# Two products of the single-layer steps without an array position, and another order of the weight loads, in an interleaved two-layer transformer kernel

## The chip, the cores and the metric

The kernel runs on one core of one Trainium2 chip. The metric is the device time of one execution in microseconds (us). A core has a matrix engine (TensorE, PE in the profile; its weight loads are shown apart, as PEld), a vector engine (VectorE, DVE), an activation engine (ScalarE, ACT), a general engine (GpSimd, POOL) and a queue engine (SyncE, SP) that here issues most of the transfers.

## What is computed

Two layers, each an attention block with a recurrent memory and a gated FFN, run over 2048 rows of 576 numbers, with the same weights in both layers. The attention goes through 64 segments of 32 rows in sequence: eight memory rows are put in front of a segment, and the first eight rows of its output are the memory of the next.

```python
def _A_ref(x, mem0, Wq, Wk, Wv, Wo, seg_len):      # H = 32 heads of 128, M = 8
    mem = mem0
    for s in range(n_seg):                          # 64 segments of 32 rows
        h = concat([mem, x[s]])                     # 40 x 576
        q, k, v = h @ Wq, h @ Wk, h @ Wv            # per head, 40 x 128
        p = softmax(where(mask, q @ k.T * scale, -1e9))
        o = (p @ v) @ Wo                            # 40 x 576
        mem = o[:M]
        outs.append(o[M:])

x = x + _A_ref(_layernorm(x), ...)                  # layer 0
x = x + (silu(ln(x) @ w1) * (ln(x) @ w3)) @ w2      # 576 -> 4608 -> 576
x = x + _A_ref(_layernorm(x), ...)                  # layer 1
x = x + (silu(ln(x) @ w1) * (ln(x) @ w3)) @ w2
```

## The kernel before

**Steps.** The recurrence makes the segments of a layer sequential. So the kernel runs the two layers side by side, layer 1 eight segments behind (`LAG = 8`): step t holds segment t of layer 0 and segment t - 8 of layer 1. There are 72 steps, 0 to 71. In steps 8 to 63 there are two layers, and the moving operand of most products is 80 columns wide (2 x 40). In steps 0 to 7 and 64 to 71 there is one, and it is 40 columns wide: these sixteen are the single-layer steps. `both(t)` tells them apart.

**A step on TensorE.** The code gives each block of products a letter. Q and q are the query and key products of one of eight units of four heads, from the 512 first rows of the model dimension and from its last 64 (four blocks of 128 rows, and a rest of 64 rows, which the kernel calls the tail). V, v, X, x, G, g are the value products. S are the scores of one of four groups of eight heads, T the transposes of the probabilities, P the product with V, O and o the product with Wo: O its first 512 output columns (32 products of 128x128), o its last 64 (8 products with 128x64 weights). F, f, W, w belong to the FFN, whose work for a group of 128 rows of each layer is spread over the next four steps; a, b, p, n are transposes.

**Order.** Nothing is scheduled on the chip. `plan` (line 76) walks a list of nodes with estimated durations and fixes the order of each engine's instructions, which engine evicts a PSUM bank, and which bank or buffer each node gets. TensorE's order is not chosen there: three strings of letters, `FIRST` (steps 0 to 15), `FOUR` (four steps, used eleven times) and `LAST` (steps 60 to 71), give it. `plan` adds `SWITCH` = 0.098 to a TensorE node whose `mode` differs from that of the node before: `full` for products on the whole 128x128 array, `col` for those placed on halves of 64 columns, `row` for halves of 64 rows, and others.

**Scores and Wo's tail.** In a two-layer step, the scores of the two layers stand on the two column halves of the array (positions (0, 0) and (0, 64)). In a single-layer step there is one layer, and its scores, with weights of 40 columns, are at (0, 0). Wo's tail has 64 output columns; `wo_tail` (line 1033) puts the heads of a group by turns on the two column halves, so that each half sums four of the eight heads:

```python
r = R64 * (hl % 2)
self.mm(yT[r:r + R64, 4, :], self.T.WO[:, self.head(g, hl), 4 * P:D], OT[:, hl, :], False, ...,
        tile_position=(0, r))
```

The two sums are added later: ScalarE copies the odd half to `YO` (`y_odd`, line 1044, node `Yodd`), and VectorE adds it to the even half when it writes the memory's last 64 rows for the next step (`y_mem`, second part) and the segment's output (`yts`, second part). The first Q of the next step waits for the first part of `y_mem` alone; the first q also for the second part.

**Transfers.** All weights of the attention stay in SBUF: Wq and Wk in `W`, loaded in two halves of 16 heads (`load_qk`), Wv in `WV`, Wo in `WO`, in four quarters of eight heads. They are issued as Wq/Wk half 0, half 1, Wv, Wo (`ld_h`, `ld_v`, `ld_o`, lines 251 to 253, where the lower number goes first). FFN weights stream through two buffers each (`W13`, `W2C`) for every four steps. After step 71 one FFN for one row group is left (18 pairs of 128 hidden columns). For two of its pairs the weights are kept from the FFN before; the other sixteen are loaded by `tail_load` (line 686) over Wq and Wk in `W` and over Wv in `WV`, in eight pieces of two pairs. A piece waits for the Q and q products of step 71 that read its part of `W`, its second part for the last value products; pieces 4 to 7 wait for the O blocks of step 71 as well (`late`, line 467). One queue (SP) issues these transfers in the order of the plan, so a transfer that waits for a buffer holds back those behind it.

`qk` (line 869) has a detail that matters at the start: in step 0, for units 0 and 4, twelve wide products with the identity run first, if the unit's main block comes before its tail block.

Of the kernel before, what the change touches and what calls it, by code (L numbers as in the profile page):

```python
# [10 lines left out]
ALU = mybir.AluOpType  # L11
# [173 lines left out]
def ewh(*ns):  # L185
# [5 lines left out]
    "maQqqqQQSQqqqQTQSqqQSQSXxvVPTPTOPOTOoooPOoQQQqqVSqqvQQqqSQQqqSQTXPSxTOPTPOTOPoooOoaQQqqqqQSvQVSqQQqTQSqqQSPTPOOT"  # L191
    "ooPTPOOooQQqqqvqSVQQQqSTQqqQPSqQOSoTXPTOPTOPxooOoQQpQqqqqQSVSnvqQFffqFQQTSqqPQOToSfFPWTOPfFTOPFOfoooWQQfqqqQSvVF"
    "qfQFQWSqqQFSfQTQPqqfFOTSoWPFTOPfxXTFPOOoooWQQqqfqQQSfqFSvVfqqQFQWSqTQQPFqffTOSoPWOTFPFTOPfaOoooWQFQqqfQSVvqqfFQQ"
    "SqWQQqqqQSTPSTbOPoXTOPTxxPOOoooXqqQpQQqqSVvnQFFSfqQqfqQQTSqfFPQTOPSofWTOPFOTFPWOoooFQqqffQQqSQQQqqgqGTSWPQQfqqFF"
    "fgSSTGGPFgfTOWPOfgGTOPFOooooWQQfqqqFQvSfqFQQfqSVTFQqfFQPSaTWQPfqqFOSoTWFOPffFTOPWOoooFQqqqfQQSWQqqQQSqqTbQSGgqgQ"
    "PGTGPSggOTGPOTOPoooOoQQppqqVqqvSQQnnQFSfqfqFTQQPFSqqfQTwOPWFSoffTOFPwTOPWOoooFQffqqFQwWSQQFfqqfFTGqqgSQPQFWTQSgf"
    "qqGQwPFTSfggOGGPOTwPOOooooWFfqqQQFQqfqvVSQQWFfqqSQwTFPaSqfqQTQwFWPSffTOPFOOTwPWOooooFqqfqQQWqSQQQSqqqQQbQSqggGTG"
    "PGTSggPGTOPOTwPOOoooo"
)
FOUR = (  # L200
    "QqQpQpQqqqvVSSnnQFffqqFQQTFSffqqQPFTWSPOwTFPOTOPwOooooWQQqqqfQSQQQqqqfFGgfSSTFPFQqfqgGQTWwPFTSfggGFPGOTOPOOooooW"
    "wQQqqqfQFQvfqfVSSwFQWQFqffqFWTQPwTFSffqqQOPWoSwTFPFOTOPwWOoooffFQqqQWQSqqqQaQSbQQTQqqqgGSSgPGTGPOTggGPOTwPOOoooo"
)
LAST = (
    "QQpqqqQpSqqQQnVqvSnQTQQPqqSFTSffOPFOTFPfwTOPFOooooWQQqfqqQFwWSfqfQQFGSgfqqQTFPGwSTWFqfgqQQPWTFSfgfgGFwGPOTOPOOoo"
    "oofFWQwQFqfqqQQWSfqVvSQFTFqqfQPQTwSqqfFOQPWwffSFTFPOOTFPWOoooowQQqqqfQQSvqqqVSQWTQQPqqQOTSSbPwvVoXTOPToxPOOooVpp"
    "qqvQQQqqSQQnnQqqfSFQTFPSfqqQTFfSPOOwTWPFfTOPFOoooowQWfqqQQQFvqqfVSSFQQfqqFTWQfqqSQPwTOPoSXfTFPOWOTxfPFOwoooFQQvq"
    "fqVSqqQQWwFTQqfqfSQQPFwFqfqSQTWOPSfFTFWPOTOPwOooooffQFqqQWQSqqqQwFvSfVQTQPWqqQSOQqwTSbPOTXoPToxPOOooQqqqqQpQQSVv"
    "QnqSQFqfqfFQTQqSPSwTOPFFTffoPOTOPwOoooFQqqfqQQqfvSVFQFQSqfqQTQQqfqSFPSXTwPOTFPOTxooPOOoowQQqqvfSVqqqQQQSqQQTSfFP"
    "FTfqqQOoSPwTfOFPFTOPfooOowQQqqqqQSQQSqfqFQVvSfFTwQQqfqPTSFPFTOPOTOPwOooooffpFnwFfffFFFwffFFwfffFFwFwfffFFFwfffFF"  # L210
    "wFwFffffFFww"
# [11 lines left out]
def make_nodes(em, nseg, pools, o=Opt, dma_bw=230e3, load_bw=400e3):  # L223
# [27 lines left out]
    ld_h = [load("ldqk", kb(512 + 2 * R64, 4096), half - 9.0, em.load_qk(half)) for half in (0, 1)]  # L251
    ld_v = [load("ldv", kb(512 + 2 * R64, 4096), -7.0, em.load_v())]
    ld_o = [load("ldo", kb(1024, 576), g - 6.0, em.load_o(g)) for g in range(NG)]
# [45 lines left out]
    def v_nodes(name, t, k, prio, tail_at, emit, strips, deps, tail_deps, free):  # L299
# [6 lines left out]
        for r in (0, 1):  # L306
            outs = em.v_parts(strips, r)
            b[r].users = len(outs)
            for p0, width, row, blk in outs:
                e = node("AD", ew(512), em.v_ev(b[r], p0, width, row, blk), deps=[m_, n] + free.get(blk // 2, []), prio=prio + 0.01 * (blk // 2),  # L310
                         rel=[b[r]], name=name + "e")
                vx_ev.setdefault((name, t, blk // 2), []).append(e)
# [17 lines left out]
    def vg_out(t, g, b, deps, row):  # L330

        return [node("AD", ew(512), em.v_ev(b[r], row, R64, row, 2 * g + r), deps=deps, prio=t + o.vm + 0.01 * g + (0.05 if row == 0 else 0.0), rel=[b[r]],
                     name="VGe") for r in (0, 1)]
# [10 lines left out]
    def step(t):  # L344
# [17 lines left out]
        for g in range(NG):  # L362
# [18 lines left out]
            sc = node("PE", 8 * 0.0165 * nl, em.scores(t, g, qs, s), deps=qe, prio=pf + o.sc, mode="col", acq=[s, sme], rel=qs, name="SC")  # L381
# [26 lines left out]
            wot = node("PE", 4 * mm80, em.wo_tail(t, g, ot), deps=[wo], prio=t + o.wo + o.wog * g, mode="col", rel=[ot], name="WOt")  # L408
# [7 lines left out]
        if t == nst - 1:  # L416
            last_reads[2].extend(wos)
# [3 lines left out]
        yo = node("ACT", actc(c80), em.y_odd(t), deps=wots[3:], prio=t - 0.008, name="Yodd")  # L421
        if nxt:
            m = 8 * len(nxt)
            ye.append(node("ACT", actc(4 * m), em.y_mem(t, nxt, 0), deps=wos[3:] + wots, prio=t - 0.01, name="Ymem"))
            ye.append(node("DVE", dve(m, m), em.y_mem(t, nxt, 1), deps=[yo] + ye, prio=t - 0.005, name="Ymem"))
        ht_mem[t + 1] += ye
        yts = [node("ACT", actc(*([128] * nl)), em.yts(t, ls, 0), deps=wos[3:] + wots + ye, prio=t + 0.01, rel=[y], name="YTS")]
        yts.append(node("DVE", dve(*([32] * nl)), em.yts(t, ls, 1), deps=[yo] + yts, prio=t + 0.01, rel=[y], name="YTSt"))
# [12 lines left out]
    last_reads = [], [], []  # L441
    kept = {}

    def job(j):
# [18 lines left out]
        if last:  # L463
            v_done, qk_done, wo_done = last_reads
            tail = []
            for i in range(8):
                late = wo_done[i - 4:i - 3] if i >= 4 else []
                parts = [(0, 9 * 512, qk_done[2 * i:2 * i + 2] + late), (1, 4 * 576, v_done + late)]
                tail.append([load("tail", kb(128, c), s0 + o.tail_at + 0.01 * i, em.tail_load(i, what), deps=dep) for what, c, dep in parts])
# [89 lines left out]
class Emitter:  # L559
# [126 lines left out]
    def tail_load(self, i, what):  # L686

        def f(n):
            T = self.T
            fa = i * 512  # L690
            t13, t2 = T.W[:, :, fa:fa + 512], T.WV[:, i * 4 * D:(i + 1) * 4 * D].rearrange("p (b d) -> p b d", b=4)
# [610 lines left out]
```

## Time and profile before

| | before |
|---|---|
| median of three runs | 2702.27 us (2697.04 to 2702.94) |
| span of the profiled run | 2703.5 us, mean granted TensorE clock 0.992 |
| TensorE busy | 2629.8 us, 97% of the span |
| VectorE, ScalarE, GpSimd busy | 2089.3, 1370.6, 333.5 us |
| transfers | 321.40 MB, mean 119 GB/s |

The page gives busy times, and a chain: the work that ended last, followed back step by step to what released it. A timeline line has start, length, engine, line, operation, written and read tiles, weight shape, the shape of the moving operand and the number of instructions merged in it; a matmul's length includes the time in which the next ones already run, so the distance between starts is the time it costs. All matmuls are recorded by one helper (line 578), so the tile names tell the groups apart: `bank<-QKT` are scores, `bank<-OT,WO` with weights of 128*64 is Wo's tail, `bank<-HT,W` Q and q, `bank<-WV,HT` values, `bank<-XTB,W` and `bank<-W2C,HTT` or `bank<-WV,HTT` the FFN.

### The profile page before, as it was taken

What the parts mean: (1) busy time and instruction counts of PE and PEld (TensorE: products, weight loads), DVE (VectorE), ACT (ScalarE), POOL (GpSimd) and SP (SyncE); (2) the same over time, 40 slices, a digit from 0 to 9 for tenths busy, and PEclk for the clock granted to TensorE, in tenths of its full rate; (3) what the DMA queues carried; (4) which work ended last, traced back from release to release, by engine and by line L of the source; (5) the groups of instructions that cost most, each with busy time, mean ns of one, the idle gap of its engine ahead of it and who ended that gap; (6) DMA issues with size and microseconds to landing.
All of it is one profiled execution on the core that took longest, in us unless ns stands there. A gap on an engine that the chain in (4) does not pass through costs nothing.

```text
span 2703.5 us, 126553 instructions
## 1 busy us (share of the span) xinstructions
PE 2629.8 (97%) x55714; PEld 2227.4 (82%) x55795; DVE 2089.3 (77%) x5376; ACT 1370.6 (51%) x4025; POOL 333.5 (12%) x400
## 2 busy tenths in 40 slices
PE   5999999999999999999999999999999999999998
PEld 3788888888888888888888888888888888888886
DVE  4778887887778778777877877787787777787876
ACT  2655554544546454454645445464544546454553
POOL 1111110110101011010101101010110101011110
PEclk7999999999999999999999999999999999999999
DMA  9064534334343333434333343433334342434358
GB/s 316 4 176 120 158 89 119 88 110 125 93 131 88 115 92 110 125 95 130 87 114 93 110 125 93 131 88 112 94 110 125 93 131 71 125 97 135 117 164 258
DMA packets 483224, 321.40 MB, mean 119 GB/s; under 512 B 26376, under 2 KB 477328, under 8 KB 482160
## 3 DMA queue, kind: packets, MB, share of 16 engines
q1 hardware_dynamic: 479488, 306.22, 38.7%
q8 instruction: 436, 7.14, 1.1%
q0 software_dynamic: 3024, 6.93, 0.9%
q14 instruction: 116, 0.95, 0.1%
q10 hardware_dynamic: 160, 0.16, 0.0%
HBM read 308.49 MB, written 2.36 MB: 115 GB/s over the span
## 4 chain that ended last, share of the span: by engine, by line
PE 87%; ACT 4%; DMA 4%; DVE 3%; issue 1%; SPq 0%; POOL 0%; DVEq 0%; ACTq 0%; POOLq 0%
PE bank L578 87%; ACT V L581 3%; DMA W<-in_B_w_dram 2%; DVE SME L584 1%; DMA W<-in_A_Wk_dram 1%; DMA WV<-in_A_Wv_dram 1%; DVE STAT L584 1%; DVE V L584 1%; ACT SME L581 0%; SPq L587 0%; DMA W2C<-in_B_w_dram 0%; ACT XTB L581 0%; ACT PTS L581 0%; ACT QKT L581 0%; DVE PB L584 0%
## 5 line engine op out<-in xcount | busy, mean ns | idle before, releaser
L578 PEld LDWEIGHTS <-W 128*128 128x128 bf16 (+1 forms) x29520 | 1238.8, 98 | 150.6 <-issue 44.2
L578 PE MATMUL bank<-HT,W 128*128 128x80 bf16 (+3 forms) x23040 | 812.4, 197 | 23.7 <-DMA W<-in_A_Wq_dram 10.5
L578 PE MATMUL bank<-XTB,W 128*128 128x256 bf16 (+3 forms) x6480 | 661.3, 261 | 8.1 <-DMA W<-in_B_w_dram 6.9
L581 ACT ACTIVATE QKT<-bank 128x256 bf16<-128x256 f32 (+3 forms) x1587 | 367.6, 318 | 372.7 <-PE bank L578 353.8
L981 POOL MEMSET PB<- 128x1024 bf16 x288 | 274.1, 952 | 1820.1 <-PE bank L578 1317.4
L578 PE MATMUL bank<-OT,WO 128*128 128x80 bf16 (+3 forms) x11520 | 407.1, 198 | 1.1 <-issue 0.5
L581 ACT ACTIVATE V<-bank 64x512 bf16<-64x512 f32 (+1 forms) x616 | 347.3, 586 | 109.4 <-PE bank L578 104.2
L578 PEld LDWEIGHTS <-WO 128*128 128x128 bf16 (+1 forms) x11520 | 379.8, 102 | 16.1 <-issue 6.0
L578 PE MATMUL bank<-WV,HT 128*32 128x512 bf16 (+5 forms) x3160 | 356.9, 385 | 13.9 <-issue 8.5
L578 PE MATMUL bank<-W2C,HTT 128*128 128x288 bf16 x2240 | 315.4, 286 | 0.3 <-DMA W2C<-in_B_w_dram 0.2
L584 DVE TENSOR_TENSOR PB<-SME,STAT 40x128 bf16<-40x128 f32 (+4 forms) x912 | 274.8, 335 | 14.9
L584 DVE TENSOR_REDUCE STAT<-SME 104x8 f32<-104x320 f32 (+1 forms) x576 | 274.0, 476 | 13.9 <-ACT SME L581 8.5
L581 ACT ACTIVATE HTT<-bank 128x512 bf16<-128x512 f32 (+1 forms) x324 | 180.0, 557 | 180.7 <-PE bank L578 178.7
L578 PEld LDWEIGHTS <-HT 128*32 128x32 bf16 (+4 forms) x3240 | 137.1, 96 | 157.0 <-issue 38.5
L584 DVE SCALAR_TENSOR_TENSOR XR<-bank,XR 128x288 f32<-128x288 f32 x576 | 246.5, 450 | 15.8 <-PE bank L578 7.9
L578 PEld LDWEIGHTS <-HTT 128*128 128x128 bf16 x2304 | 209.8, 98 | 49.1 <-issue 0.9
L581 ACT ACTIVATE OT<-bank 128x320 bf16<-128x320 f32 (+1 forms) x398 | 149.7, 406 | 167.9 <-PE bank L578 166.5
L584 DVE CAST QKT<-bank 128x192 bf16<-128x192 f32 (+2 forms) x461 | 124.9, 317 | 137.7 <-PE bank L578 136.2
L584 DVE SCALAR_TENSOR_TENSOR HTT<-HTT,bank 128x512 bf16<-128x512 bf16 (+1 forms) x324 | 202.5, 625 | 33.7 <-ACT HTT L581 29.6
L584 DVE TENSOR_TENSOR HTT<-HTT,bank 128x512 bf16<-128x512 bf16 (+1 forms) x324 | 203.6, 628 | 30.6 <-DVE HTT L584 0.5
L581 ACT ACTIVATE PTS<-bank 128x320 bf16<-128x320 f32 (+1 forms) x385 | 144.9, 403 | 161.6 <-PE bank L578 123.9
L581 ACT ACTIVATE SME<-SME 104x320 f32<-104x320 f32 (+1 forms) x288 | 135.9, 472 | 138.1 <-DVE SME L584 135.6
(61 smaller groups left out, 1804.4 us busy)
## 6 DMA issues: line engine op xcount, KB each, us to landing
W<-in_B_w_dram SPq DMA_DIRECT2D x612, 256.0 KB, 3.6
W2C<-in_B_w_dram SPq DMA_DIRECT2D x306, 288.0 KB, 3.3
W<-in_B_w_dram SPq DMA_DIRECT2D x612, 32.0 KB, 3.3
W<-in_B_w_dram SPq DMA_DIRECT2D x16, 512.0 KB, 8.8
WO<-in_A_Wo_dram SPq DMA_DIRECT2D x4, 1152.0 KB, 16.1
XR<-in_A_x_dram POOLq DMA_DIRECT2D x16, 288.0 KB, 2.9
WV<-in_B_w_dram SPq DMA_DIRECT2D x8, 576.0 KB, 7.3
W<-in_A_Wq_dram SPq DMA_DIRECT2D x8, 512.0 KB, 8.7
```

The costliest lines, as they stand in the source:

```text
L578: self.ch("PE", self.nc.tensor.matmul(out, lhsT=lhsT, rhs=rhs, start=start, stop=stop, skip_group_check=True, **k))
L581: self.ch("ACT", self.nc.scalar.activation(*a, **k))
L584: self.ch("DVE", getattr(self.nc.vector, fn_)(*a, **k))
L981: return lambda n: self.ch("POOL", self.nc.gpsimd.memset(self.T.PB[:, pb.i], 0.0))
```

## The change

It has five parts.

1. In single-layer steps the scores and Wo's tail are written without a tile position, and the plan takes them as `full`. All eight heads of a group of Wo's tail are then summed in one half, so the copy to `YO` goes, and the additions become copies.
2. Wv is loaded between the two halves of Wq and Wk, and Wo after them.
3. The tail weights of the last FFN come in four pieces of four pairs instead of eight of two, without the wait for step 71's O blocks.
4. The plan's estimates change: the eviction of values from 0.49 and 0.60 us (ScalarE, VectorE) to 0.55 and 0.60, and the scores.
5. `FIRST`, `FOUR` and `LAST` are written anew for this plan, so the order of the blocks changes in all steps.

The purpose of the first part is to take changes of the array's mode, which the plan charges, out of the single-layer steps; of the second, to have values and the first softmaxes done while weights still arrive; of the third, to start the last weights sooner.

```diff
-    ld_h = [load("ldqk", kb(512 + 2 * R64, 4096), half - 9.0, em.load_qk(half)) for half in (0, 1)]
-    ld_v = [load("ldv", kb(512 + 2 * R64, 4096), -7.0, em.load_v())]
-    ld_o = [load("ldo", kb(1024, 576), g - 6.0, em.load_o(g)) for g in range(NG)]
+    ld_h = [load("ldqk", kb(512 + 2 * R64, 4096), 3 * half - 9.0, em.load_qk(half)) for half in (0, 1)]
+    ld_v = [load("ldv", kb(512 + 2 * R64, 4096), -8.0, em.load_v())]
+    ld_o = [load("ldo", kb(1024, 576), g - 5.0, em.load_o(g)) for g in range(NG)]
...
-                e = node("AD", ew(512), em.v_ev(b[r], p0, width, row, blk), ...
+                e = node("AD", (0.55, 0.6), em.v_ev(b[r], p0, width, row, blk), ...
...
-            sc = node("PE", 8 * 0.0165 * nl, em.scores(t, g, qs, s), ..., mode="col", ...
+            sc = node("PE", 8 * (0.0185 * nl if nl == 2 else 0.025), em.scores(t, g, qs, s), ..., mode="col" if nl == 2 else "full", ...
...
-            wot = node("PE", 4 * mm80, em.wo_tail(t, g, ot), ..., mode="col", rel=[ot], name="WOt")
+            wot = node("PE", (4 if nl == 2 else 8) * mm80, em.wo_tail(t, g, ot), ...,
+                       mode="col" if nl == 2 else "full", rel=[ot], name="WOt")
...
-        yo = node("ACT", actc(c80), em.y_odd(t), deps=wots[3:], prio=t - 0.008, name="Yodd")
+        yo = [node("ACT", actc(c80), em.y_odd(t), deps=wots[3:], prio=t - 0.008, name="Yodd")] if nl == 2 else []
...
-            for i in range(8):
-                late = wo_done[i - 4:i - 3] if i >= 4 else []
-                parts = [(0, 9 * 512, qk_done[2 * i:2 * i + 2] + late), (1, 4 * 576, v_done + late)]
+            for i in range(4):
+                parts = [(0, 9 * 1024, qk_done[4 * i:4 * i + 4]), (1, 8 * 576, v_done)]
...
-                                True, True, tile_position=(0, 64 * kd))
+                                True, True, **({"tile_position": (0, 64 * kd)} if both else {}))
...
+                if not self.both(t):
+                    self.mm(yT[0:R64, 4, :], self.T.WO[:, self.head(g, hl), 4 * P:D], OT[:, hl, :], False, g == NG - 1 and hl == GH - 1)
+                    continue
                 r = R64 * (hl % 2)
...
+                        if self.both(t):
+                            self.v("tensor_tensor", o..., pick(yT[0:R64, 4]), pick(self.T.YO[:, 0:nq]), op=ALU.add)
+                        else:
+                            self.v("tensor_copy", o, pick(yT[0:R64, 4]))
```

## The prediction

> **What bounds the kernel now.** I read the page's busy shares and its chain first, then windows over one repeat of the four-step cycle, then the chain in order of time at both ends, and last the TensorE timeline of single-layer steps.
>
> ```profile
> PE 2629.8 (97%) x55714; PEld 2227.4 (82%) x55795; DVE 2089.3 (77%) x5376; ACT 1370.6 (51%) x4025; POOL 333.5 (12%) x400
> PE 87%; ACT 4%; DMA 4%; DVE 3%; issue 1%; SPq 0%; POOL 0%; DVEq 0%; ACTq 0%; POOLq 0%
> ...
> 1143.60:1301.08 157.48, 156.12 (x3120) 132.59 (x3126) 123.58 (x315) 80.89 (x239) 18.55 (x22) 1.00 0.37 108
> ```
>
> TensorE is the bound: 87% of the chain. The window row is one pass through FOUR (length, then PE, PEld, DVE, ACT, POOL, the clock, the DMA share, GB/s). I added up the gaps from one matmul start to the next there, and took off each product's own period and 0.095 us for each change of tile shape: about 3 us of the 157.5 are stalls, of which 1.7 come from the VG products and one step end that both orders keep. So the eleven repeats hold little to win.
>
> ```profile
> 6.87 10.33 DMA W<-in_A_Wk_dram
> 17.22 12.72 DMA W<-in_A_Wk_dram
> 29.95 16.16 DMA WV<-in_A_Wv_dram
> ...
> 59.44 1.61 PE bank L578 x39
> ...
> 2673.53 10.34 DMA W<-in_B_w_dram
> ...
> 2686.52 8.00 DMA W<-in_B_w_dram
> ...
> 2694.57 3.69 PE bank L578 x50
> ```
>
> The ends are bound by transfers: step 0 follows the weights until Wo's last quarter is used at 59.44, and the last FFN follows its weights until 2694.57.
>
> ```profile
> 2616.65 0.35 PE L578 MATMUL bank<-ident,PB 104*128 104x40 bf16 x8
> 2616.94 0.37 PE L578 MATMUL bank<-QKT 128*40 128x40 bf16 x8
> 2617.24 0.29 PE L578 MATMUL bank<-XTB,W 64*128 64x128 bf16 x4
> ...
> 2602.80 0.43 PE L578 MATMUL bank<-OT,WO 128*64 128x40 bf16 x16
> 2603.17 0.37 PE L578 MATMUL bank<-PTS,V 128*128 128x40 bf16 x8
> 2603.38 2.12 PE L578 MATMUL bank<-OT,WO 128*128 128x40 bf16 x80
> ```
>
> Single-layer prices, from starts. Eight transposes take 0.29 to the scores' start: 8 x 0.025 and 0.09 for the change of tile shape. The scores take 0.30: again 8 x 0.025 and 0.10. Sixteen tail products of Wo take 0.37 with one change, 17 ns each, because two of them, on the two halves of the array, share a period of 32 ns. PV takes 0.21 to WO, where the shape doesn't change: 8 x 0.025.
>
> **What the Trainium skill says.** "TensorEngine Tiling (Array Packing)", Key Properties: changing the tiling mode, not just the tile, drains the TensorE. The trace agrees: 0.09 to 0.10 us at each change, and none between the halves. "TensorE: Matmul & The Clock Gate", section "Wait — 56ns, not 53.3ns?": start to start never falls below about 25 ns, however few the columns; the single-layer products show exactly 25. Its section on LDWEIGHTS prices a weight load at P/1.2 ns, 53 ns for 64 columns; the trace has no run of 64-column loads into one and the same tile, only the pairs at 32 ns.
>
> **The change part by part.**
>
> *Scores without a position.* The plan books them as "full", with no change of shape. But in both built programs each product carries a tile size, and a product without a position gets the smallest tile that holds its weights: 40 columns give 128x64 at position 0, field for field what the explicit position gave before. I take it that these 512 products run as before, changes of shape included: 0 us.
>
> *Wo's tail without a position.* All eight products of a group now carry 128x64 at position 0, where they alternated between 0 and 64. The pairing goes. In 64 groups (16 single-layer steps by 4) the first to the last start spans 119 ns (median of before). After, seven periods: at least 7 x 25 = 175, at most 7 x 53 = 371. I take 7 x 32 = 224, since a tile gets its next 64 columns every 32 ns in the pairs. That is 0.105 us a group, 64 x 0.105 = 6.7 us on TensorE (3.6 to 16). In steps 4 to 7 and 64 to 70 FFN products fill the gaps, and TensorE is nearly the whole chain, so it counts in full; steps 1 to 3 and 71 hide part. I count 5.7.
>
> *Changes of shape.* Counted over the built TensorE streams: 1296 before, 1300 after (322 to 329 in FIRST, 65 in each FOUR as before, 259 to 256 in LAST). 4 x 0.095 = 0.4 us. Had the two kinds really become 128x128 products, it would be 1191.
>
> *YO.* Sixteen ScalarE copies of 0.20 us go, and VectorE copies instead of adding. The next step's first QK waits for the 128-row memory copy alone (61.07 to 61.32 in the chain), and its tail products, which wait for the rest, come at least 1.3 us of TensorE work later in nearly every step: 0.
>
> *Load order.* The same 18.9 MB arrive before Wo's last quarter, which landed at 58.15 and was used at 59.44. V's products and the first two softmaxes move ahead of the second half of Wq and Wk. Against that, the twelve 512-column warm-up products move from unit 0 to unit 4 (only a unit whose main block comes first has them, and unit 0 now begins with its tail), when TensorE is no longer waiting, and two tail groups instead of one end the step. I take 0, within 1 us either way.
>
> *New order strings, V evictions dearer in the plan.* In FOUR the engines trade six Q/K evictions (14 to 20 on VectorE, some 4 us, so VectorE goes from 78 to 81% of the cycle). I measured both orders in TensorE work: the shortest transpose-to-PV and PV-to-WO distances stay 0.98 us, scores to transposes 5.7 against 6.0, but reuses of a bank within 0.98 us go from seven to twelve. What has to fit is an eviction (0.44 to 0.49) and two handovers. I add 0.1 us a cycle, 1 us. In the single-layer steps the distances widen: step 67 had PV to WO and the end to the next QK at zero and stalled 0.5 and 0.7 us there, and now has 0.8 or more at both; step 1's zero transpose-to-PV distance (a 1.1 us stall) becomes 0.45. Before lost some 9 us in such latency waits in steps 1 to 7 and 4 in 64 to 71. I take 4 back.
>
> *Tail weights in four pieces.* The sync queue issues in order, and what it is stuck behind is the W2C load that waits for the second-last W2b group of the FFN before; 10.6 MB of tail weights stand behind that wait in both versions. In TensorE work from the start of step 71, that group ends at 17.4 us instead of 21.5, so the stream starts about 4 us sooner, at the same rate (323 GB/s over 2658 to 2696). But the last piece now feeds four FFN pairs instead of two, and its W comes last: the TensorE work behind the last landing grows from 2.8 us (W2's last piece landed at 2696.1, the last product started at 2698.9) to 4 x 0.86 for the up products, 0.8 for their tails and the changes, and 2.6 for three down groups, 6.7. Gain 4, loss 4: 0.
>
> Sum: 5.7 + 0.4 + 0 + 1 - 4 + 0 = +3 us, 2705 us.
>
> **The rivals.**
>
> *The intended effect.* If a product without a position doesn't drain the array, 105 changes go: -10.0; the unpaired tail at 25 ns adds 3.6, the orders give 3 back: 2693. For it: the order was planned so. Against it: the tile sizes are the same fields as before, and the explicit position-0 scores paid 0.09 to 0.10 at each change.
>
> *The order wins more.* The stalls before step 12 and after step 59 sum to some 22 us at each end, DMA waits included. If the new order wins back 10 of them instead of 4, and the tail's earlier start outweighs its coarser piece by 3, it is 5.7 + 0.4 + 1 - 10 - 3 = -6: 2696. For it: the plan's V eviction cost was 0.49 and is now 0.55 on ScalarE, where the trace has 0.59, and a narrow step has up to 16 of them. Against it: transposes to PV in step 2 stay at zero distance.
>
> *Unpaired weight loads cost 53 ns.* 64 x 0.252 = 16 us, less the 4: 2714.
>
> *The new FOUR stalls.* 1 us a cycle from the tighter banks, times 11, on top of the sum: about 2714.
>
> **How the numbers follow.** Forecast 0.41; order wins more 0.20; intended effect 0.10; dear loads 0.14; FOUR stalls 0.15. Within 0.2% is 2696.9 to 2707.7: three quarters of the forecast case (0.31) and 0.07 of the second and third case, 0.38. Faster: the rest of those, 0.23, and 0.03 of the forecast's lower edge, 0.26. Slower: the dear loads and stalls, 0.29, and 0.07 of the forecast's upper edge, 0.36. The range takes in the cases at 2693 and at 2714, with the 6 us that before's three runs spread: 2692 to 2717.
>
> **What would show it.** In the profile after, the single-layer score groups should still show 0.09 to 0.10 us at both their edges and 25 ns inside; if QKT products of 40 columns follow the transposes after 0.2 us, the intended effect is there. The eight products OT,WO 128*64 of a single-layer group should stand 32 ns apart, not 4 and 28 by turns; 25 or 53 moves the sum to its bounds. A FOUR cycle should take 157.2 to 158; 159 is the stall case. First QK of step 1 near 61, the last tail weights landing some 4 us earlier against the end of step 71, and 6 to 7 us of TensorE work after it. If the single-layer steps are shorter than before in spite of the unpaired tails, my 4 us for the order was too little.

## The result and the profile after

The changed kernel takes 2731.64 us (2727.68 to 2733.30, four runs), the kernel before in the same series 2700.82 (2697.04 to 2702.94, four runs): a ratio of 1.0114, 95% interval 1.0096 to 1.0131, some 31 us slower. The forecast was 2705, with a range up to 2717. The two profiled executions have spans of 2703.5 and 2725.9, so the traces show 22.4 us of it.

The page of the kernel after, its busy times and its chain:

```profile
PE 2643.1 (97%) x55722; PEld 2236.9 (82%) x55795; DVE 2137.9 (78%) x5551; ACT 1343.6 (49%) x3834; POOL 333.7 (12%) x400
...
PE 88%; DVE 6%; DMA 2%; issue 1%; ACT 1%; SPq 1%; DVEq 0%; ACTq 0%
```

TensorE is busy 13.3 us longer. VectorE has 175 instructions and 48.6 us more and is 6% of the chain instead of 3%; ScalarE has 191 fewer. So evictions have moved from ScalarE to VectorE.

I matched each block of both orders with its products in the trace and took the time of the first QK (or its tail) of a step. The table is worked out from the traces: the start before, and how much later the step starts in other kernels (the experiments below are named by what they change). "End" is the end of the last product.

```
step   before    after   before+products'   before+all     after, three
                         numbers (E14)      numbers (E19)  put back (E20)
   1     61.3     +4.9        +0.5             -0.1            +1.8
   4    128.5     +7.2        +7.1             +2.5            +3.5
   8    240.4     +8.3        +9.7             +5.5            +3.8
  12    373.2    +10.2       +14.1            +11.1            +4.1
  16    530.7    +11.6       +14.3            +11.9            +5.6
  32   1161.0    +12.4       +19.3            +23.3            +6.4
  60   2265.9    +11.0       +25.1            +40.4            +6.5
  66   2490.5     +5.3       +26.0            +42.6            -1.6
  70   2606.4    +17.8       +28.2            +43.6           +10.1
  71   2631.4    +20.5       +28.2            +44.4           +10.0
 end   2699.2    +22.5       +30.6            +47.3           +10.2
```

In the column of after, 4.9 us are lost before step 1, 7 more up to step 16, nothing in the eleven passes through FOUR, and 11 from step 60 on. How these 11 fall on single steps can't be read from the table, because the new LAST moves FFN work across step 66: in steps 60 to 65 after runs 724 FFN products where before runs 784, in steps 66 to 69 it runs 516 where before runs 432. One caution on such curves: E7 below differs from before only in the last FFN's transfers, and its profiled execution is 4.7 us ahead at step 8 and stays about 5 us ahead up to step 71. Single executions spread that much in the first steps; only the timed ratios decide.

The chain of the kernel after in order of time, at its start:

```profile
14.97 16.84 DMA WV<-in_A_Wv_dram
...
37.17 0.68 DVE V L583
37.87 0.69 DVE V L583
38.57 0.69 DVE V L583
...
39.29 0.88 DVE SME L583 x2
...
42.66 0.70 DVE V L583
43.38 0.55 DVE PB L583 x2
...
47.26 7.38 PE bank L577 x146
...
66.23 3.78 PE bank L577 x153
```

Wv now lands at 31.8, as intended. But V's evictions stand in VectorE's queue ahead of the first softmax, which begins at 39.29; another V eviction stands before its last step at 43.38. TensorE's transposes wait for that until 43.98. And from 46.44 to about 51 run the twelve warm-up products of unit 4, most of them in the 7.38 us from 47.26. In the kernel before they ran from 11.30 on, while TensorE was waiting for weights. The first QK of step 1 starts at 66.23 instead of 61.32.

The chain at the end:

```profile
2702.94 9.40 DMA W<-in_B_w_dram
2712.34 0.05 issue
2712.38 8.35 PE bank L577 x97
...
2720.74 0.92 PE bank L577 x6
```

The last weights land 60.4 us after the first QK of step 71 (2712.34 against 2651.9) instead of 63.1 (2694.52 against 2631.4), 2.7 us sooner. Behind them stand 8.35 + 0.92 = 9.3 us of TensorE instead of 3.69 + 0.92 = 4.6.

TensorE's timeline in single-layer steps of the kernel after:

```profile
2635.90 0.37 PE L577 MATMUL bank<-QKT 128*40 128x40 bf16 x8
2636.20 0.97 PE L577 MATMUL bank<-HT,W 128*128 128x40 bf16 x32
...
2643.85 0.68 PE L577 MATMUL bank<-OT,WO 128*64 128x40 bf16 x16
2644.47 0.37 PE L577 MATMUL bank<-PTS,V 128*128 128x40 bf16 x8
```

The scores still take 0.30 us to the next start: 8 x 0.025 and one change of shape. At every edge of such a group with a full product the median gap is 109 to 112 ns, as before. Sixteen tail products take 0.62 to the next start instead of 0.37. Inside a group they stand 32 ns apart, and from the first to the last start of eight there are 242 ns at the median instead of 119.

The softmax holds TensorE up more than before. From step 1 on, its idle time ahead of the transposes of the probabilities (`bank<-ident,PB`) that ended when VectorE had written PB sums to 0.9 us before and 9.0 after.

### The profile page after: what moved, and what is told of

The parts are those of the page before. It is cut to its first block, busy times and chain, and to the rows that moved or that the text cites. A ratio compares the mean times of both kernels' runs of the same rounds, so it can differ in the third digit from the quotient of the medians.

```text
span 2725.9 us, 126469 instructions
## 1 busy us (share of the span) xinstructions
PE 2643.1 (97%) x55722; PEld 2236.9 (82%) x55795; DVE 2137.9 (78%) x5551; ACT 1343.6 (49%) x3834; POOL 333.7 (12%) x400
## 4 chain that ended last, share of the span: by engine, by line
PE 88%; DVE 6%; DMA 2%; issue 1%; ACT 1%; SPq 1%; DVEq 0%; ACTq 0%
PE bank L577 88%; DVE STAT L583 2%; SPq L586 1%; DVE SME L583 1%; DVE V L583 1%; DMA W<-in_B_w_dram 1%; DVE PB L583 1%; DMA WV<-in_A_Wv_dram 1%; ACT V L580 0%; DVE OT L583 0%; DVE PTS L583 0%; DMA W<-in_A_Wk_dram 0%; ACT QKT L580 0%; DMA W2C<-in_B_w_dram 0%; ACT SME L580 0%
## 5 line engine op out<-in xcount | busy, mean ns | idle before, releaser
L577 PEld LDWEIGHTS <-W 128*128 128x128 bf16 (+1 forms) x29520 | 1238.4, 98 | 144.8 <-issue 48.6
L580 ACT ACTIVATE QKT<-bank 128x64 bf16<-128x64 f32 (+4 forms) x1451 | 345.2, 311 | 399.2 <-PE bank L577 378.7
L577 PE MATMUL bank<-OT,WO 128*128 128x80 bf16 (+3 forms) x11520 | 412.9, 198 | 0.9 <-issue 0.5
L577 PEld LDWEIGHTS <-WO 128*128 128x128 bf16 (+1 forms) x11520 | 385.8, 102 | 14.2 <-issue 3.5
L577 PE MATMUL bank<-WV,HT 128*32 128x512 bf16 (+4 forms) x3169 | 356.6, 386 | 15.6 <-DMA WV<-in_A_Wv_dram 8.5
L583 DVE CAST QKT<-bank 128x192 bf16<-128x192 f32 (+2 forms) x597 | 162.9, 318 | 116.0 <-PE bank L577 113.9
L583 DVE CAST V<-bank 64x512 bf16<-64x512 f32 (+1 forms) x259 | 177.4, 685 | 33.0 <-PE bank L577 26.9
## 6 DMA issues: line engine op xcount, KB each, us to landing
W<-in_B_w_dram SPq DMA_DIRECT2D x8, 1024.0 KB, 13.3
```

Source lines behind the costliest of these rows:

```text
L577: self.ch("PE", self.nc.tensor.matmul(out, lhsT=lhsT, rhs=rhs, start=start, stop=stop, skip_group_check=True, **k))
L580: self.ch("ACT", self.nc.scalar.activation(*a, **k))
L583: self.ch("DVE", getattr(self.nc.vector, fn_)(*a, **k))
```

## The experiments

The experiments stand in five groups, by what they ask; their numbers have gaps. All ratios are to the kernel before on the same chip, with 95% intervals; 0.1% is 2.7 us. In the diffs, a line of "..." marks what is left out.

**The parts one by one.** E1 is the kernel before with the unpaired tails alone:

```diff
             for hl in range(GH):
+                if not self.both(t):
+                    self.mm(yT[0:R64, 4, :], self.T.WO[:, self.head(g, hl), 4 * P:D], OT[:, hl, :], False, ...)
+                    continue
...
-        yo = node("ACT", actc(c80), em.y_odd(t), ...)
+        yo = [node("ACT", actc(c80), em.y_odd(t), ...)] if nl == 2 else []
```

> The kernel before with one part of the change: in the single-layer steps Wo's last 64 columns are products without a position, and YO goes with the pairs. Order strings, loads, tail weights and the scores stay as before. Theory A (the new order costs most of the 29 us): 64 groups x 0.125 us = 8 us at most, 6 to 8 slower than before, so about 2708, and the rest of the growth is not here. Theory B (the lost pairs cost most, because each step of the recurrence is longer and its other waits do not shrink): 15 us or more slower, 2716 to 2730.

Measured: 2709.68 us, ratio 1.0020 (1.0012 to 1.0028), 5.4 us. Theory B falls: the recurrence doesn't multiply it. E2 is the complement, the kernel after with the pairs and YO back (the same lines the other way round):

> The kernel after with the pairs and YO put back, everything else of the change kept. Theory A: it keeps the cost of order, loads and tail pieces and loses only the 6 to 8 us of the lost pairs: about 2723, 0.8% slower than before. Theory B: it comes back to within 8 us of before, 2702 to 2710.

Measured: 2726.82, ratio 1.0086 (1.0072 to 1.0100). So 23 of the 31 us have nothing to do with the products: order, loads, tail pieces and plan.

E3 puts the warm-up products back to unit 0, in FIRST of the kernel after:

```diff
-    "maqQQQQqqqxvXSSVTPTPQqqQQqqSQSOoTOPToPOO...
+    "maQqQQQqqqxvXSSVTPTPqQqQQqqSQSOoTOPToPOO...
```

> The kernel after with two letters of FIRST swapped twice, so that the main block of unit 0 again comes first, and with it the twelve warm-up products; nothing else. Theory A (the warm-up products run at 46.4 to 51.8 us, after the weights have landed, and that is the 4.9 us that step 1 starts later): step 1 starts about 4.5 us sooner, at 61 to 62, and the whole is 3 to 5 us shorter than after. Rival (the start is bound by the later landing of Wq, Wk and Wo): step 1 starts within 1 us of after's 66.2.

Measured: 2725.74, ratio 1.0089 (1.0072 to 1.0106), by the ratios 7 us less than after, though the intervals overlap. Step 1 starts at 63.6, 2.6 us sooner than in after; the waits for the softmax behind V's evictions stay. So the place of these products explains about half of the 4.9 us at the start.

E7, the last FFN's weights in four pieces, alone in the kernel before (`range(4)`, 1024 columns a piece, no `late`, as in the change):

> The kernel before with one part of the change: the last FFN's weights in four pieces. Forecast's step (4 us gained by the earlier start, 4 lost behind the last piece): within 1.5 us of before, and the end of step 71 to the end of the kernel as before. Rival (the coarse piece costs more than the earlier start gives): 2 to 4 us slower, all of it after the first QK of step 71.

Measured: 2705.83, ratio 1.0009 (1.0002 to 1.0016): 2.4 us slower, and in its trace the stretch from the first QK of step 71 to the last product is 4.4 us longer. The rival fits better, but by the interval, 0.5 to 4.3 us, the forecast's 1.5 isn't excluded.

**Strings.** Two hybrids put whole strings of the kernel before into the kernel after (each string has the same number of each letter in both). E4 takes FIRST and the order of the loads:

```diff
-FIRST = (...)    # of after
+FIRST = (...)    # of before
...
-    ld_h = [load("ldqk", ..., 3 * half - 9.0, ...)]
+    ld_h = [load("ldqk", ..., half - 9.0, ...)]
```

> The kernel after with FIRST and the order of the weight loads of before; FOUR, LAST, the unpaired tails and the tail pieces of after. Theory A splits its loss into a start (steps 0 to 15: 11.6 us in the profiles, of which some 3.5 are unpaired tails of steps 0 to 7) and an end (about 11): this kernel should win back about 8, to 2723, with the first QK of step 1 near 61 again, and its loss after step 59 should be that of after. Theory B: nothing comes back beyond 2 us, since the tails are still unpaired.

Measured: 2728.71, ratio 1.0092 (1.0079 to 1.0105), by the ratios 6 us less than after, with overlapping intervals. Step 1 starts at 60.3 again, 1 us sooner than in the kernel before. Then 5.5 us go up to step 8 (near the spread of single executions) and 6.3 more up to step 12, with TensorE's order of the kernel before, in which the unpaired tails alone (E1) have cost 1.2 by then. The loss of the start and the loss of the steps after it are two things, and the second isn't in the string.

E5 takes LAST of before instead.

> The kernel after with LAST of before; FIRST, FOUR, load order, unpaired tails and tail pieces of after. Theory A: of the 11 us that the profiles show from step 60 to the end, 4 are unpaired tails of steps 64 to 71; the order string gives back 4 to 7, to about 2725. Rival (the end is bound by the four coarse tail pieces and by the unpaired tails, not by the string): within 2 us of after.

Measured: 2730.86, ratio 1.0101 (1.0088 to 1.0114), not separable from after. With LAST of before, the trace loses 9.8 us from step 60 to the end, where after loses 11.5. The rival fits: of the 9.8, the four pieces took 4.4 in E7's trace and the unpaired tails 1.4 in E1's, so some 4 us (an estimate from single traces) are left for something else.

**The planner's numbers.** What E4 and E5 have in common is the rest of the plan: the change also gave `plan` other durations. It doesn't choose TensorE's order, but it does choose which engine evicts a bank, and the order in the queues of ScalarE and VectorE. First V's evictions alone, put back in after (E6) and put into before (E11):

```diff
-e = node("AD", ew(512), em.v_ev(...), ...)
+e = node("AD", (0.55, 0.6), em.v_ev(...), ...)
```

> The kernel after with one thing put back: V's evictions cost the planner 0.49 and 0.60 us again, as before, so that it shares evictions between ScalarE and VectorE as before did; all three order strings, loads, unpaired tails and tail pieces stay. In the last runs FIRST of before inside the kernel after still lost 10 us between steps 8 and 14, with the same order on TensorE as before. Theory V (the planner's dearer V evictions move other evictions to VectorE, whose queue then delays the softmax): 8 to 15 us come back, to about 2718. Theory S (the strings themselves are longer): within 2 us of after.

> The kernel before with one thing of the change: V's evictions cost the planner 0.55 on ScalarE and 0.6 on VectorE. The TensorE order, loads and products are those of before. Theory V: 10 to 18 us slower, 2712 to 2720, lost in steps 8 to 14 and from step 60 on. Theory S: within 2 us of before.

Measured: E6 2728.12, ratio 1.0097 (1.0082 to 1.0113), by the ratios 4.6 us less than after with overlapping intervals, so neither theory's figure. E11 2714.51, ratio 1.0052 (1.0037 to 1.0067): 14 us, from two numbers in the plan, with the same products, loads and order on TensorE. Its trace is 10.7 us behind at step 12 and loses nothing after that. Since TensorE's order is the same, one wait can be laid beside the other. Transposes of the last group of step 1: VectorE, ScalarE and TensorE of the kernel before (each the timeline of one engine):

```profile
78.51 0.48 DVE L584 TENSOR_TENSOR SME<-SME,STAT 40x320 f32<-40x320 f32 x1
79.03 0.68 DVE L584 CAST V<-bank 32x512 bf16<-32x512 f32 x1
79.74 0.33 DVE L584 CAST PTS<-bank 128x160 bf16<-128x160 f32 x1
79.98 0.47 DVE L584 TENSOR_REDUCE STAT<-SME 40x8 f32<-40x320 f32 x1
...
80.79 0.54 DVE L584 TENSOR_TENSOR PB<-SME,STAT 40x64 bf16<-40x64 f32 x2
81.26 0.80 DVE L584 BATCH_NORM_STATS2 LNS<-XN 128x6 f32<-128x288 bf16 x2
```

```profile
79.12 0.46 ACT L581 ACTIVATE SME<-SME 40x320 f32<-40x320 f32 x1
79.48 0.29 ACT L581 ACTIVATE PTS<-bank 128x160 bf16<-128x160 f32 x1
79.79 0.59 ACT L581 ACTIVATE V<-bank 32x512 bf16<-32x512 f32 x1
```

```profile
81.48 0.35 PE L578 MATMUL bank<-ident,PB 104*128 104x40 bf16 x8 [0.30 <-DVE PB L584]
```

The same place in the kernel before with the new V cost:

```profile
79.47 0.48 DVE L584 TENSOR_TENSOR SME<-SME,STAT 40x320 f32<-40x320 f32 x1
...
80.22 0.68 DVE L584 CAST V<-bank 32x512 bf16<-32x512 f32 x1
80.83 0.80 DVE L584 BATCH_NORM_STATS2 LNS<-XN 128x6 f32<-128x288 bf16 x2
81.66 0.21 DVE L584 BATCH_NORM_AGGREGATE LNS<-LNS 128x2 f32<-128x12 f32 x1
81.91 0.15 DVE L584 TENSOR_SCALAR LNS<-LNS 128x1 f32<-128x1 f32 x1
81.98 0.47 DVE L584 TENSOR_REDUCE STAT<-SME 40x8 f32<-40x320 f32 x1
...
82.75 0.43 DVE L584 TENSOR_SCALAR XN<-XN,LNS 128x576 bf16<-128x576 bf16 x1
83.21 0.18 DVE L584 COPY XN<-XN 128x64 bf16<-128x64 bf16 x1
83.30 0.54 DVE L584 TENSOR_TENSOR PB<-SME,STAT 40x64 bf16<-40x64 f32 x2
```

```profile
80.03 0.59 ACT L581 ACTIVATE V<-bank 32x512 bf16<-32x512 f32 x1
80.65 0.50 ACT L581 ACTIVATE PTS<-bank 128x160 bf16<-128x160 f32 x2
81.03 0.46 ACT L581 ACTIVATE SME<-SME 40x320 f32<-40x320 f32 x1
```

```profile
83.99 0.42 PE L578 MATMUL bank<-ident,PB 104*128 104x40 bf16 x8 [1.74 <-DVE PB L584]
```

The softmax's subtraction ends near 79.0 in the first and 79.95 in the second. Before, the exponential follows it on ScalarE in 0.1 us, and the sum and the probabilities (PB) stand in VectorE's queue ahead of the normalisation of the next rows (BATCH_NORM). With the new numbers a V eviction and two PTS evictions stand ahead of the exponential (81.03), and the normalisation, in two pieces, ahead of the sum and of PB (83.30). From the end of the subtraction to PB's start it is 1.8 us before and 3.35 now, and TensorE waits 1.74 us where it waited 0.30. None of these ScalarE and VectorE instructions is longer than before; what differs is which engine takes some of the evictions, and the places in the two queues. "TensorE: Matmul & The Clock Gate", section "Architectural detail: the array is 16× 32×32, not 1× 128×128", in the Trainium skill says that the queues of ScalarE and VectorE are strictly first in, first out; the two timelines agree with that.

The granted TensorE clock, which the trace records over time, has a share as well. In steps 1 to 7 it is 0.5 instead of 1.0 for 10.9 us in the trace of before, and for 21.0 in that of E11 (20.5 in E14 and 23.9 in E16 below). How much of the loss this is wasn't separated. In after it is 6.8 us there, and 17.0 against 14.3 from step 1 to the end, so it explains little of the loss of after.

E14, the other numbers: the scores and tails of the single-layer steps booked as after books them, and nothing else:

```diff
-sc = node("PE", 8 * 0.0165 * nl, ..., mode="col", ...)
+sc = node("PE", 8 * (0.0185 * nl if nl == 2 else 0.025), ..., mode="col" if nl == 2 else "full", ...)
...
-wot = node("PE", 4 * mm80, ..., mode="col", ...)
+wot = node("PE", (4 if nl == 2 else 8) * mm80, ..., mode="col" if nl == 2 else "full", ...)
```

> The kernel before with three of the planner's numbers of after and nothing else: single-layer scores and Wo's tails are booked without a change of shape, scores at 25 ns a product, tails at eight periods instead of four. Products, TensorE order, loads and V's eviction costs are those of before. Theory V (any change of the planner's numbers without a new fit of the strings reorders the queues of ScalarE and VectorE, and softmax work ends up behind normalisation and V evictions): 5 to 12 us slower, in single-layer and narrow steps. Rival (only V's eviction cost does that): within 2 us of before.

Measured: 2729.95, ratio 1.0098 (1.0083 to 1.0113): 26 us, almost as much as the whole change, and more than twice what I expected. By the table 14 are lost up to step 12, and 11 in the passes through FOUR, one a pass, where I had expected none.

E19, all of after's numbers in the kernel before:

> The kernel before with all of the planner's numbers of after (V's evictions, scores and tails) and nothing else. The two alone cost 14 and 26 us. If they add: 40 us, about 2742. If each only disturbs a fit of numbers and strings that can be lost just once: 15 to 30 us, 2717 to 2732, no more than the larger of the two.

Measured: 2750.47, ratio 1.0182 (1.0168 to 1.0195): 49 us. The two costs add, and a little more; by the table 28.5 us of it now lie in FOUR. Part of that is the clock: the trace has seven stretches of 3.41 us in FOUR in which the granted clock is 0.5, one each in seven of the eleven passes. These seven take 160.8 to 161.1 us, the other four 159.2 to 159.9, so such a stretch costs some 1.65 us, about 12 us in all. All eleven passes have the same two waits of 0.85 and 0.82 us on TensorE, 14.2 and 15.2 us after their start; the stretches begin between 15.3 and 16.3 us, and what decides whether one follows isn't shown. The traces of before, E14 and after have no such stretch in FOUR. The kernel after has these numbers too and loses nothing in FOUR. So its FOUR fits its numbers, as the old FOUR doesn't.

E16, the same numbers as in E14, but the plan is first made with the old numbers, and each eviction keeps the engine that it had there:

```diff
+    old = make_nodes(em, nseg, pools)    # with the numbers of before
+    plan(old, pools, ORDER)
...
+    for a, n in zip(old, nodes):
+        if n.eng == "AD":
+            n.eng, n.dur = a.by, n.dur[a.by == "DVE"]
```

> The kernel before with the planner's numbers of after for the scores and tails (which cost 26 us by themselves), but each eviction stays on the engine that it had before: the planner is run with the old numbers first, and only who evicts is taken from it; the order in the queues is that of the new numbers. If the assignment is the cause (more evictions on VectorE delay the softmax): within 5 us of before, about 2706. If the order within the two queues is the cause: 15 us or more stay, 2717 to 2730.

Measured: 2717.72, ratio 1.0057 (1.0042 to 1.0073). Between the two: 11 of the 26 us go with who evicts, and 15 stay. Who evicts is not the whole cause. The 15 need not all be the order inside the queues: `plan` also picks the bank or buffer of each node by its estimated times, and this run lets that change too.

E17, the kernel after with all the numbers of before:

> The kernel after with all of the planner's numbers of before (V's evictions, and the scores and tails booked as four periods each with a change of shape); its order strings, products, loads and tail pieces stay. If the numbers are wrong in themselves: 10 us or more come back, 2721 or less. If numbers and strings only fit as a pair, and the strings of after are the longer ones with either: within 4 us of after, 2727 to 2735.

Measured: 2724.98, ratio 1.0082 (1.0068 to 1.0096), 8.6 us less than after; the two intervals just meet. Also between: the numbers of after cost its own strings about 9 us; with the old numbers its strings are still the longer ones. The waits for the softmax stay as well: ahead of the transposes of PB, TensorE idles 7.4 us from step 1 on, against 9.0 in after and 0.9 before. On its VectorE, QKT is evicted 593 times, as against 597 in after and 461 in before: that shift comes with the strings, not with the numbers.

**Real full-array products.** The change books the single-layer scores and tails on the full array, but a product with 40 or 64 weight columns still changes the shape. What would it bring if they were really on it? E8 has scores with 80 weight columns (this head's 40 and the next head's), tails with Wo's last 128 columns, in the kernel before. The copies that write the scores' weights put the heads next to each other for this (not shown):

```diff
-self.mm(S[0:QW, ...], Q[:, q0:q0 + QW], ...)
+self.mm(S[0:2 * QW, ...], Q[:, QW * hl:QW * (hl + 2)], ...)
...
-self.mm(yT[r:r + R64, 4, :], self.T.WO[:, head, 4 * P:D], ...)
+self.mm(yT[:, 4, :], self.T.WO[:, head, D - P:D], ...)
```

> The kernel before, in which the single-layer scores and Wo's tails really use the full array: the scores with 80 weight columns (the head's 40 and the next 40, whose results nobody reads), the tails with WO's last 128 columns (the upper half is read, the lower half repeats chunk 3). Order strings, loads and tail weights of before. Changes of tile shape by count 1188 instead of 1296. Theory (a product's tile follows from its number of columns, and each change of shape costs 0.095 us): 108 x 0.095 = 10.3 us less, 64 tails at 25 ns instead of 17 cost 3.6, so about 2696, 6.7 us faster. Rival (a product without a position never drained the array, and 128 columns only make the loads dearer): no gain, 2702 to 2712.

Measured: 2703.39, ratio 1.0009 (1.0001 to 1.0018). The changes of shape are gone: the gap ahead of a score group falls from 109 to 25 ns. But the products inside stand 38 to 39 ns apart, which by 64 x 7 x 13.5 ns takes 6 us of the gain back. E13, with 128 columns:

> As the kernel of 80 weight columns, but with 128 columns (the head's 40 and the next 88, whose results nobody reads) for the single-layer scores; Wo's tails again with WO's last 128 columns; order strings, loads and tail weights of before. In the run with 80 columns the changes of shape were gone (25 ns at the scores' edge instead of 109), but its products stood 38 to 39 ns apart instead of 25. Theory (80 columns load more slowly than 128): the score products return to 25 ns, 64 x 7 x 13.5 ns = 6 us come back, about 2697, 4 to 7 us faster than before. Rival (a weight load costs by its columns, so 128 are dearer than 80): 50 to 60 ns apart, 2708 or more.

Measured: 2703.00, ratio 0.9999 (0.9990 to 1.0008). The products are as expected; the timeline of the two kernels, first 80 and then 128 columns:

```profile
2606.09 0.50 PE L578 MATMUL bank<-QKT 128*80 128x40 bf16 x8
```

```profile
2569.11 0.37 PE L578 MATMUL bank<-QKT 128*128 128x40 bf16 x8
2569.32 0.36 PE L578 MATMUL bank<-PTS,V 128*128 128x40 bf16 x8
```

Eight products of 128 columns take 0.21 us to the next start, edge included, where those of before take 0.30. And yet nothing comes out faster than before. E18, the scores alone on 128 columns, pairs and YO kept:

> The kernel before with the single-layer scores alone on 128 weight columns; the tails keep their pairs, and YO stays. 57 changes of shape fewer, 5.4 us on TensorE, none of the 3.6 us that unpaired tails cost. If TensorE's time counts in full: about 2697, 5 us faster than before. If half of it is taken up by waits for the softmax, as the kernel with both on 128 columns suggests (13.4 us less than with unpaired tails of 64 columns by count, 5.7 by the runs): 2 to 3 us faster.

Measured: 2702.26, ratio 1.0000 (0.9992 to 1.0008). Of the 5.4 us by count at most some 2 reach the end. ScalarE and VectorE run the same instructions in the same order as before, and the copies with the new layout take 0.305 us as before, so these don't eat the gain. E15, the products of E13 in the kernel after:

> The kernel after, with its single-layer scores and tails on 128 weight columns, so that the planner's booking (no change of shape) comes true: 1191 changes of shape instead of 1300, and tails 25 ns apart instead of 32. Theory: 109 x 0.095 = 10.4 and 64 x 7 x 7 ns = 3.1, 13.5 us less than after, about 2718; what is left above before, some 17 us, is order and queues. Rival (the lost time of after is mostly that its planner books products that the chip does not run, so that all its waits shift): within 5 us of before.

Measured: 2725.55, ratio 1.0078 (1.0063 to 1.0093), some 10 us less than after where 13.5 were counted. So even with the effect that its plan books, the changed kernel is 21 us slower than before.

**Three causes at once.** E20 is the kernel after with the warm-up products first, the pairs and YO back, and the old numbers (E3, E2 and E17 in one):

> The kernel after with three things put back together: the warm-up products at unit 0 (alone 5 us), the pairs of Wo's tail with YO (alone 5 us), and all of the planner's numbers of before (alone 7 us). Its order strings otherwise, its load order and its four tail pieces stay. If these causes are separate and add, 17 of the 29 us come back: about 2714, 12 us slower than before, left for the strings, the load order and the tail pieces. If the strings of after need their own numbers once the products are paired again, less than 8 us come back: 2724 or more.

Measured: 2715.95, ratio 1.0053 (1.0040 to 1.0067). From 1.0114 that is 16.5 us back, with some 6 us of play by the two intervals. The 5, 5 and 7 us of the expectation are differences of medians from different series; by the ratios the three alone are 7 (E3), 8 (E2) and 9 us (E17), 23 together. So the three bring back about half of the loss; whether they add in full or overlap a little, these runs can't tell. TensorE's waits for PB from step 1 on are still 7.4 us here.

## Why the prediction was wrong

*Bound and method.* TensorE is still the bound (88% of the chain), and FOUR loses nothing: right, with the 1 us that I added there not needed.

*Scores without a position.* Right: shape changes of 109 to 112 ns at their edges, 25 ns inside.

*Wo's tail.* Right in mechanism and size: 32 ns from product to product, 0.123 us a group instead of 0.105, and 5.4 us (3.2 to 7.6) in E1 where I had counted 5.7. The price of 53 ns for 64 columns in the Trainium skill ("TensorE: Matmul & The Clock Gate", LDWEIGHTS) isn't what the products take at the full granted clock; the measured 32 decides. It does appear where the granted clock is 0.5: there they stand 53 to 55 ns apart (at the full clock some 32 of 440 gaps are 52 to 53 ns). The floor of 25 ns that the prediction quotes holds here inside one tile: across the two halves, the pairs of before start 4 and 28 ns apart by turns.

*Load order.* I took 0, within 1 us; in the trace the first QK of step 1 is 4.9 us later. I had named the warm-up products and priced them at nothing; they account for about half. The rest, by the trace (no run tests it alone), is a wait that I didn't look for: V's evictions stand ahead of the first softmax in VectorE's queue. I had only asked when weights land, not what is evicted first once they are there.

*Tail weights in four pieces.* I set gain 4 against loss 4. The trace of after has 2.7 sooner and 4.6 more behind, 9.3 us of TensorE where I had 6.7; alone in the kernel before it costs 2.4 us (0.5 to 4.3). The mechanism holds; both terms were mis-sized, and against the change.

*New order strings, V evictions dearer in the plan.* This is the step that failed. I forecast -4 in the single-layer steps and +1 in FOUR. E2 has order, loads, pieces and plan together at 23 us; less some 5 for the start and 2.4 for the pieces, about 16 remain for this step. I measured distances between blocks in TensorE's order, which did widen, and took a wider distance for a shorter wait. But a wait of TensorE here isn't just an eviction and two handovers; it takes in whatever stands in the queues of ScalarE and VectorE ahead of the softmax. Where I took 4 us of waits back, TensorE's waits for PB alone, from step 1 on, grew from 0.9 to 9.0 us. Those queues are made by the plan from its durations, and I had read the change of durations as bookkeeping: I counted six evictions that change engine in FOUR, and never looked at the order inside the queues in the single-layer steps. E14 and E11 show that these numbers, with TensorE's order untouched, cost 26 and 14 us in the kernel before; E16, that the choice of engine explains less than half of the 26. In the kernel after the durations are about half of the 16 us (8.6 in E17). The other half stays with the old durations, and 7.4 us of the waits for PB stay with it; so it comes with the new strings or with what the plan makes of them.

*Rivals.* The stall case of FOUR adds up to 2715 or 2716, not 2714 (11 us on top of 2705, with the 1 us already booked or without); FOUR shows no such stall. The rival that the intended effect comes true fell as well. With products that really keep the shape, E13 and E18 gain nothing on the kernel before, and E15 wins back 10 of the 31 us.

What stays open: with three causes put back, 14 us remain (E20), of which the tail pieces may be 2.4. In its trace 10.2 us remain: 5.6 before step 16 and about 4 from step 60 on. TensorE waits 6.5 us longer for PB than in before, so much of the rest is still softmax waits, now with the old durations; which part of the new strings, the load order or the choice of banks makes them I haven't separated. Open too is where the time saved on the scores goes in E18.

## What to carry to other kernels

Where a planner fixes the queues from estimated durations, an estimate is part of the program: compare the instruction order on every engine, not on the bound one alone, and look first at what stands ahead of the short chain that the bound engine waits for. An order that was fitted to one set of estimates can lose more with another than the whole change was meant to gain (E19); but a new pair of order and estimates isn't the better one for that (E17), so price each part alone. Time saved on the bound engine need not reach the end (E18); that it only lengthens a wait for another engine is likely, but not shown here.

## What the runs showed of the hardware

The start-to-start period of products with a moving operand of 40 columns depends on the weight columns, and not in one direction. At the full granted clock it is 25 ns with 40 (before and after), 32 with 64 into the same tile (after), 38 to 39 with 80 (E8), and 25 again with 128 (E13). In the stretches at a granted clock of 0.5 the same products stand 33 to 35, 53 to 55, 66 to 69 and 32 to 34 ns apart. "TensorE: Matmul & The Clock Gate", section "Weight-path perf modes — Fast Weight Load (FWL) and DoubleRow", in the Trainium skill says that a faster load of weights is on when their number is 128; the step back from 38 to 25 agrees with it. So a product padded to 128 weight columns is cheaper than one padded to 80, and it needs no change of shape beside other full products (25 ns at the edge instead of 109).

A stretch of 3.41 us at a granted clock of 0.5 made a pass through FOUR some 1.65 us longer, and such stretches came right behind two TensorE waits of under 1 us each, in seven passes of eleven (E19). So two kernels are compared by these stretches as well as by their waits.
